# A linear-attention scan and its FFN on one core: the first six stages as a list of interleaved steps, loads held behind FFN groups, k and r of stage 0 in float32

## The chip, the core and the metric

The kernel runs on one core of a Trainium2 chip. The core has a tensor engine (PE, whose weight loads the profile lists apart as PEld), a vector engine (DVE), a scalar engine (ACT), GpSimd (POOL) and a sync engine (SP); each works off its own instructions in order. DMA transfers are issued by SP, ACT or POOL. The metric is the device time of one execution in microseconds; for the kernel before, three runs were taken.

## What is computed

An RWKV-5 style recurrence over 768 tokens for 4 batches and 8 heads of width 48, then a two-layer FFN with leaky ReLU (384 to 2048 to 384) on the 3072 tokens:

```python
for t in range(S):
    cur = np.einsum('bhd,bhe->bhde', u[None] * kt, vt)
    y[:, :, t] = np.einsum('bhd,bhde->bhe', rt, state + cur)
    state = w[None, :, :, None] * state + np.einsum('bhd,bhe->bhde', kt, vt)
...
h = x @ w_in
g = np.maximum(0.01 * h, h)
return g @ w_out
```

Inputs and output are float32.

## The kernel before

The tokens are cut into chunks of 128: 6 chunks in each of 4 batches, 24 *stages* in all, numbered 0 to 23. Weights stay in SBUF. Each stage goes through these steps, most of them one function of the kernel:

- Load: `load_stage(n)` issues three DMAs from POOL's queue, k, r and v of the chunk, float32 in memory and bfloat16 in SBUF.
- `prep(n)` (DVE, lines 267 and 269): k times a table `ktab` of powers of w, r times `qtab`, into `qk`. From stage 6 on (`TURNED`), a DMA transpose on SP's queue turns `qk` into `tp` (line 272).
- `prep2(n)` (DVE, lines 279 to 285): k times u, times r, summed over each head, times v, into `vs` (the diagonal term with u).
- `turn(n)`, stages 0 to 5 only: PE turns `qk` by eight products with an identity into two PSUM banks (line 299), k half first, and ACT copies each half to `tp` (line 305).
- `a_mm(n)` (PE, line 316): the scores, into `ps_at`; `a_mask(n)` (DVE, line 324): times the causal mask, into `at`, two operations.
- `kv_mm(n)` (PE, line 334) and `state(n)` (DVE, lines 346 to 351): the state at the end of the chunk. The last chunk of a batch has none. Its decay table `wl` comes from ACT (lines 253 and 256).
- `y_mm(n)` (PE, line 380), 40 products (28 in the first chunk of a batch), needs `at`, `vs`, `tp` and the state; ACT copies the result to `xT` (line 390).
- `g1(n, grp)`, four *FFN groups* per stage: 12 products on PE (line 401) into one of four PSUM banks, then the leaky ReLU on ACT (line 406). The four banks go round between `turn`, `g1` and `g2`.
- `g2(n)`: 16 products on PE (line 415), a copy on ACT (line 421), the output DMA on SP (line 423).

`Sched.add` records an operation with the keys it reads and writes; each engine then runs its operations in the order in which they were recorded, and waits come from the latest recorded writer of a key. A key that has no writer yet gives no wait. The order of the recording is written out by hand: lines of calls for stages 0 to 5, in blocks (a stage's attention as a whole, then FFN groups), and a loop for stages 6 to 23. The three DMAs of a later load read the key `("pace", n - 6, 0)`, which group 0 of `g1(n - 6)` writes. They are all recorded ahead of `g1_all(5)`:

```python
    for n in range(7, NST):
        load_stage(n, pace=[("pace", n - 6, 0)])
    stage_in(7)
    g1_all(5)
```

In the text a step is named by a letter and its stage: P `prep`, Q `prep2`, T `turn`, A `a_mm`, M `a_mask`, K `kv_mm`, S `state`, Y `y_mm` with its copy, G `g1` (G0.2 is group 2 of stage 0), H `g2`, L `load_stage`.

Of the kernel before, what the change touches and what calls it, by code (L numbers as in the profile page):

```python
# [111 lines left out]
def bass_rwkv5_eagle__then__act_leaky_relu_kernel(  # L112
# [63 lines left out]
    def load_w():  # L176
        def small():
            with nc.allow_non_contiguous_dma(reason="columns of w"):
                return SP.dma_start(wcol[0:D, :], dram(w, 0, [[1, D], [2 * D, NP]]))

        def small2():
            with nc.allow_non_contiguous_dma(reason="columns of w"):
                return SP.dma_start(wcol[64:64 + D, :], dram(w, D, [[1, D], [2 * D, NP]]))

        add("sp", lambda: SP.dma_start(lnw[:, :], dram(w, 0, [[0, 128], [1, HD]])), W=["lnw"], dma="lnw")
        add("sp", lambda: SP.dma_start(u_f[:, :], dram(u, 0, [[0, 128], [1, HD]])), W=["u_f"], dma="u")
        add("sp", small, R=["wcol0"], W=["wcol"], dma="wc")
        add("sp", small2, R=["wcol0"], W=["wcol2"], dma="wc2")

# [38 lines left out]
    load_stage(1)  # L228
    load_stage(2)
    for g in range(3):  # L230
        load_win(g)
    load_stage(3)
    load_win(3)
    load_stage(4)
    for i in range(4):
        load_wout(i)
    load_stage(5)
    load_stage(6)
# [9 lines left out]
    add("dve", lambda: V.tensor_copy(u_tab[:, :], u_f[:, :]), R=["u_f"], W=["u_tab"])  # L248

# [14 lines left out]

    def prep(n):
        iq = n % NQK
        add("dve", lambda: V.tensor_tensor(qk[iq][:, H:2 * H, 0:D], hd(k_sb[:, n, :]), hd(ktab[:, :]), ALU.mult),  # L267
            R=[("k", n), "ktab", ("qk0", iq)], W=[("kp", iq)])
        add("dve", lambda: V.tensor_tensor(qk[iq][:, 0:H, 0:D], hd(r_sb[:, n, :]), hd(qtab[:, :]), ALU.mult),
            R=[("r", n), "qtab", ("qk0", iq)], W=[("qp", iq)])  # L270
# [6 lines left out]
    def prep2(n):  # L277
        i2, iv = n % 2, n % NVS
        add("dve", lambda: V.tensor_tensor(ku[i2][:, :], k_sb[:, n, :], u_tab[:, :], ALU.mult),
            R=[("k", n), "u_tab"], W=[("ku", i2)])  # L280
        add("dve", lambda: V.tensor_tensor(rku[i2][:, :], r_sb[:, n, :], ku[i2][:, :], ALU.mult),
            R=[("r", n), ("ku", i2)], W=[("rku", i2)])
        add("dve", lambda: V.tensor_reduce(s_tok[i2][:, :], hd(rku[i2][:, :]), AX.X, ALU.add),  # L283
            R=[("rku", i2)], W=[("s", i2)])
        add("dve", lambda: V.tensor_tensor(hd(vs[iv][:, :]),  # L285
                                           v_sb[:, n, :].rearrange("p (h e) -> p h e", e=E)[:, :, 0:D],
                                           s_tok[i2][:, :].unsqueeze(2).to_broadcast([128, H, D]), ALU.mult),
            R=[("v", n), ("s", i2)], W=[("vs", iv)])

    def turn(n):  # L290
        it, iq = n % NTP, n % NQK
        for half in (1, 0):
            pb = bank[0] % 4
            bank[0] += 1

            def emit(half=half, pb=pb):
                for p in range(NP):
                    h0 = half * H + 2 * p
                    last = PE.matmul(ps_g[pb][:, 128 * p:128 * p + 128],  # L299
                                     qk[iq][:, h0:h0 + 2, :].rearrange("p h e -> p (h e)"), ident[:, :],  # L300
                                     start=True, stop=True)
# [3 lines left out]
            add("act", lambda half=half, pb=pb: A.activation(  # L305
                tp[it][:, NP * half:NP * half + NP, :].rearrange("p m t -> p (m t)"), ps_g[pb][:, :], AF.Copy),
                R=[("ps_g", pb)], W=[("tp", it, half)])
# [257 lines left out]
```

## Time and profile before

| | us |
|---|---|
| median of 3 runs | 189.87 |
| lowest and highest | 189.8, 190.95 |
| the profiled execution, its own time | 192.09 |
| its span, first to last instruction | 190.3 |

| engine | busy us in the span | share |
|---|---|---|
| PE | 167.7 | 88% |
| PE weight load | 132.0 | 69% |
| DVE | 103.7 | 54% |
| ACT | 92.3 | 48% |
| POOL | 70.0 | 37% |

The chain of work that ended last is 83% PE, 7% DMA, 5% ACT and 2% DVE. A line number is that of the kernel before. In a row of the profile, `out<-in` names what is written and read, `x8` is a count, and what stands in brackets behind a row is the idle time before it and what ended that.

### The profile page before, as it was taken

Reading aid. Unit: us, or ns where it says so; the run is one execution under the profiler, and the core shown is the slowest. Engines: PE = TensorE matmul, PEld = TensorE weight load, DVE = VectorE, ACT = ScalarE, POOL = GpSimd, SP = SyncE. Lnnn points to the kernel's source line nnn. Section 1 sums busy time; section 2 is a strip of 40 time slices with the busy share of each in tenths; the row PEclk is TensorE's granted clock in tenths of the full one; section 3 lists DMA queues with packets and bytes.
Section 4 is the critical chain, followed back from the end, with each engine's and each line's share of the span. In section 5 each row is a group of like instructions: output and inputs, shape, how many; then the busy total and the mean of one; then the engine's idle time right before and its main releaser. Section 6 shows DMA issues by size and latency. Waiting matters only on the chain.

```text
span 190.3 us, 6193 instructions
## 1 busy us (share of the span) xinstructions
PE 167.7 (88%) x2768; PEld 132.0 (69%) x2768; DVE 103.7 (54%) x240; ACT 92.3 (48%) x164; POOL 70.0 (37%) x87
## 2 busy tenths in 40 slices
PE   0266697789798599999999999999999999999993
PEld 0145596687475488778877877887788778778851
DVE  5498810880566665955675577558645955240000
ACT  2732277665344165356436643653475356436621
POOL 7999996059999999800000000000000000000000
PEclk9999999999999789999999999999999999999999
DMA  4999999999999999999937413430442146201112
GB/s 66 124 142 180 170 185 198 145 136 79 154 107 195 150 169 142 168 168 152 156 58 100 100 40 61 100 85 15 100 96 75 28 96 71 70 3 45 41 45 83
DMA packets 101786, 20.46 MB, mean 108 GB/s; under 512 B 94848, under 2 KB 101760, under 8 KB 101760
## 3 DMA queue, kind: packets, MB, share of 16 engines
q0 software_dynamic: 78592, 10.23, 82.8%
q1 hardware_dynamic: 23168, 9.84, 27.3%
q8 instruction: 22, 0.36, 0.9%
q14 instruction: 4, 0.03, 0.0%
HBM read 20.84 MB, written 4.72 MB: 134 GB/s over the span
## 4 chain that ended last, share of the span: by engine, by line
PE 83%; DMA 7%; ACT 5%; DVE 2%; issue 1%; SPq 0%; DVEq 0%; ACTq 0%; POOLq 0%
PE ps_g L401 34%; PE ps_g L415 32%; PE ps_y L380 9%; PE ps_at L316 5%; DMA tp<-qk 4%; ACT tp L305 3%; DMA k_sb<-in_k_dram 3%; PE ps_kv L334 2%; DVE at L324 2%; PE ps_g L299 1%; ACT xT L390 1%; ACT out_sb L421 1%; ACT gT L406 0%; DVE qk L267 0%; SPq L423 0%
## 5 line engine op out<-in xcount | busy, mean ns | idle before, releaser
L401 PE MATMUL ps_g<-xT,w_in_sb 128*128 128x128 bf16 x1152 | 71.0, 224 | 0.8 <-ACT xT L390 0.8
L401 PEld LDWEIGHTS ps_g<-xT,w_in_sb 128*128 128x128 bf16 x1152 | 68.8, 100 | 3.7 <-ACT xT L390 0.8
L415 PE MATMUL ps_g<-w_out_sb,gT 128*128 128x384 bf16 x384 | 66.1, 326 | 0.0
L406 ACT ACTIVATE gT<-ps_g 128x512 bf16<-128x512 f32 x96 | 57.3, 597 | 14.2 <-PE ps_g L401 7.1
L324 DVE TENSOR_TENSOR at<-ps_at,mask 128x512 bf16<-128x512 f32 x48 | 30.9, 686 | 58.0 <-PE ps_at L316 58.0
L415 PEld LDWEIGHTS ps_g<-w_out_sb,gT 128*128 128x128 bf16 x384 | 36.2, 98 | 22.6
L421 ACT ACTIVATE out_sb<-ps_g 128x384 f32<-128x384 f32 x24 | 11.8, 490 | 57.0 <-PE ps_g L415 57.0
L198 POOL DMA_DIRECT2D k_sb<-in_k_dram x24 | 24.1, 1002 | 9.6 <-PE ps_g L401 8.8
L198 POOL DMA_DIRECT2D v_sb<-in_v_dram x24 | 24.2, 1008 | 0.0
L198 POOL DMA_DIRECT2D r_sb<-in_r_dram x24 | 24.0, 1001 | 0.0
L390 ACT ACTIVATE xT<-ps_y 128x384 bf16<-128x384 f32 x24 | 11.8, 490 | 19.6 <-PE ps_y L380 19.4
L380 PE MATMUL ps_y<-at,v_sb 128*32 128x128 bf16 x384 | 16.0, 234 | 2.9 <-DVE at L324 2.9
L316 PE MATMUL ps_at<-tp 48*128 48x128 bf16 x192 | 10.2, 229 | 8.0 <-ACT tp L305 5.6
L380 PE MATMUL ps_y<-ident,vs 128*32 128x128 bf16 x288 | 15.9, 233 | 0.0
L380 PEld LDWEIGHTS ps_y<-at,v_sb 128*32 128x32 bf16 x384 | 10.8, 101 | 6.0 <-DVE at L324 3.6
L285 DVE TENSOR_TENSOR vs<-v_sb,s_tok 128x384 bf16<-128x384 bf16 x24 | 13.4, 558 | 0.8
L283 DVE TENSOR_REDUCE s_tok<-rku 128x8 f32<-128x384 bf16 x24 | 13.3, 553 | 0.8
L316 PEld LDWEIGHTS ps_at<-tp 48*128 48x128 bf16 x192 | 5.8, 98 | 11.4 <-ACT tp L305 6.9
L380 PE MATMUL ps_y<-tp,st 128*32 128x128 bf16 x240 | 13.3, 228 | 0.0
L299 PE MATMUL ps_g<-ident,qk 128*128 128x128 bf16 x48 | 5.1, 264 | 8.0 <-DVE qk L267 8.0
L380 PEld LDWEIGHTS ps_y<-ident,vs 128*32 128x32 bf16 x288 | 10.7, 104 | 0.0
L299 PEld LDWEIGHTS ps_g<-ident,qk 128*128 128x128 bf16 x48 | 3.7, 117 | 8.8 <-issue 8.1
(35 smaller groups left out, 93.5 us busy)
## 6 DMA issues: line engine op xcount, KB each, us to landing
out_dram<-out_sb SPq DMA_DIRECT2D x24, 192.0 KB, 2.2
k_sb<-in_k_dram POOLq DMA_DIRECT2D x24, 96.0 KB, 10.4
r_sb<-in_r_dram POOLq DMA_DIRECT2D x24, 96.0 KB, 10.9
v_sb<-in_v_dram POOLq DMA_DIRECT2D x24, 96.0 KB, 11.8
w_in_sb<-in_moe_w_in_dram POOLq DMA_DIRECT2D x4, 384.0 KB, 8.0
w_out_sb<-in_moe_w_out_dram POOLq DMA_DIRECT2D x4, 384.0 KB, 12.6
tp<-qk SPq DMA_TRANSPOSE x18, 4.5
lnw<-in_w_dram SPq DMA_DIRECT2D x1, 192.0 KB, 4.2
```

What stands on the lines that cost most here:

```text
L198: add("pool", lambda: G.dma_start(dst, src), R=pace, W=[(which, n)], dma=f"{which}{n}")
L283: add("dve", lambda: V.tensor_reduce(s_tok[i2][:, :], hd(rku[i2][:, :]), AX.X, ALU.add), R=[("rku", i2)], W=[("s", i2)])
L285: add("dve", lambda: V.tensor_tensor(hd(vs[iv][:, :]), v_sb[:, n, :].rearrange("p (h e) -> p h e", e=E)[:, :, 0:D], s_tok[i2][:, :].unsque ...
L299: last = PE.matmul(ps_g[pb][:, 128 * p:128 * p + 128], qk[iq][:, h0:h0 + 2, :].rearrange("p h e -> p (h e)"), ident[:, :], start=True, sto ...
L316: last = PE.matmul(ps_at[hh][:, 128 * p:128 * p + 128], tp[it][rows, NP + p, :], tp[it][rows, p, :], start=True, stop=True)
L324: add("dve", lambda hh=hh: V.tensor_tensor(at[n % NAT][:, hh, :, :], ps_at[hh][:, :].rearrange("p (m i) -> p m i", i=128), mask[:, :].unsq ...
L380: last = PE.matmul(ps_y[32 * q:32 * q + 32, 128 * s:128 * s + 128], a, m, start=first_mm, stop=last_mm)
L390: add("act", lambda: A.activation(xT[n % NXT][:, :, :].rearrange("p s t -> p (s t)"), ps_y[:, 0:HD], AF.Copy), R=["ps_y"], W=[("xT", n % N ...
L401: last = PE.matmul(ps_g[pb][:, 128 * f:128 * f + 128], w_in_sb[:, s, 128 * fb:128 * fb + 128], xT[n % NXT][:, s, :], start=s == 0, stop=s ...
L406: add("act", lambda: A.activation(gT[n % NG][:, 4 * grp:4 * grp + 4, :].rearrange("p f t -> p (f t)"), ps_g[pb][:, :], AF.Lrelu), R=[("ps_ ...
L415: last = PE.matmul(ps_g[pb][:, 0:HD], gT[n % NG][:, s, :], w_out_sb[:, s, :], start=s == 0, stop=s == NFB - 1)
L421: add("act", lambda: A.activation(out_sb[io][:, :], ps_g[pb][:, 0:HD], AF.Copy), R=[("ps_g", pb)], W=[("o", io)])
```

## The change

Four things change.

1. The calls for stages 0 to 5 become a list of steps, `ORDER`, recorded from left to right; the loop for stages 6 to 23 records the same steps as before. The first loads become a list too, `LOADS`, with parts of w_in earlier, among the loads of stages 1 to 3.
2. `load_stage(n)` of stages 8 to 23 is recorded behind the FFN groups of stage n - 6 (`L8` to `L11` in the list, the others in the loop), so that the key it reads has a writer. The loads of stages up to 7 have no hold.
3. k and r of stage 0 go to two new float32 tiles, k by SP's queue, r by ACT's; `prep(0)` and `prep2(0)` read those.
4. Smaller ones: the second half of `turn(0)` is copied by DVE; the decay table is computed behind the first half's copy and followed by the load of ACT's table for the leaky ReLU; the copy of u to bfloat16 moves into `prep2(0)`.

```diff
+FIRST, LAG, LOADED = 6, 2, 7
+LOADS = """k1 r1 v1 wi0 wi1 k2 r2 wi2 v2 wi3 k3 r3 v3 wo0 wo1 k4 r4 v4 wo2 wo3 k5 r5 v5 k6 r6 v6 k7 r7 v7"""
+ORDER = """
+P0 K0 T0 Q0 A0 S0 P1 M0 T1 Q1 P2 K1 A1 Y0 M1 G0.0 T2 S1 G0.1 Y1 G0.2 Q2 G1.0 A2 G1.1 M2 K2 P3 G1.2 Y2 T3 S2 G0.3 K3 G1.3
...
-    load_w()
-    load_one(0, "k")
+    add("sp", lambda: SP.dma_start(lnw[:, :], dram(w, 0, [[0, 128], [1, HD]])), W=["lnw"], dma="lnw")
+    load_first("k")
+    add("sp", lambda: SP.dma_start(u_f[:, :], dram(u, 0, [[0, 128], [1, HD]])), W=["u_f"], dma="u")
+    load_wcol(0)
+    load_wcol(1)
...
+            if n == 0 and half == 0:
+                add("dve", lambda dst=dst, pb=pb: V.tensor_copy(dst, ps_g[pb][:, :]),
+                    R=[("ps_g", pb)], W=[("tp", it, half)])
...
+    def decay_table():
+        add("act", lambda: A.activation(wcol[:, :], wcol[:, :], AF.Ln), R=["wcol0", "wcol", "wcol2"], W=["wcol"])
...
+        add("act", lambda: A.preload_act_table(AF.Lrelu))
+
     def state(n):
+        if n == 0:
+            decay_table()
...
+    steps = {"P": prep, "Q": prep2, "T": turn, "A": a_mm, "M": a_mask, "K": kv_mm, "S": state, "Y": y_part,
+             "G": g1, "H": g2, "L": lambda n: load_stage(n, pace=[("pace", n - 6, 0)])}
+    for name in ORDER.split():
+        steps[name[0]](*(int(x) for x in name[1:].split(".")))
+    for n in range(FIRST, NST):
         for grp in range(4):
             g1(n, grp)
...
+        if n + 6 > LOADED and n + 6 < NST:
+            load_stage(n + 6, pace=[("pace", n, 0)])
```

Three places show what the list does to an engine's order. The first is PE behind Y2: in the kernel before, the first FFN products (`xT,w_in_sb`, nine groups of 12 in one piece) follow, then T3, A3, K3 and three more groups.

```order
L401 MATMUL ps_g<-xT,w_in_sb 128x128 x108
L299 MATMUL ps_g<-ident,qk 128x128 x8
L316 MATMUL ps_at<-tp 128x128 x8
L334 MATMUL ps_kv<-v_sb,qk 128x96 x4
L401 MATMUL ps_g<-xT,w_in_sb 128x128 x36
```

The same place, behind Y2, in the kernel after: T3, G0.3, K3, G1.3, A3, then G2.0 and G2.1.

```order
L308 MATMUL ps_g<-ident,qk 128x128 x8
L426 MATMUL ps_g<-xT,w_in_sb 128x128 x12
L347 MATMUL ps_kv<-v_sb,qk 128x96 x4
L426 MATMUL ps_g<-xT,w_in_sb 128x128 x12
L329 MATMUL ps_at<-tp 128x128 x8
L426 MATMUL ps_g<-xT,w_in_sb 128x128 x24
```

So single FFN groups now stand between a turn, the scores and the state product of one stage; six groups (G0.0 to G0.2 and G1.0 to G1.2) have gone ahead of this place. At the very start of PE's order the kernel after has K0, T0, A0, T1, K1, A1 and then Y0, where before Y0 came ahead of T1.

The second place is DVE from P0 to the first mask (`at0`). Before:

```order
L267 TENSOR_TENSOR qk0<-k_sb,ktab 128x8x48
L269 TENSOR_TENSOR qk0<-r_sb,qtab 128x8x48
L279 TENSOR_TENSOR ku0<-k_sb,u_tab 128x384
L281 TENSOR_TENSOR rku0<-r_sb,ku0 128x384
L283 TENSOR_REDUCE s_tok0<-rku0 128x8
L285 TENSOR_TENSOR vs0<-v_sb,s_tok0 128x384
L324 TENSOR_TENSOR at0<-ps_at0,mask 128x512
```

After:

```order
L274 TENSOR_TENSOR qk0<-k0_f,ktab 128x8x48
L276 TENSOR_TENSOR qk0<-r0_f,qtab 128x8x48
L316 CAST tp0<-ps_g1 128x512
L286 CAST u_tab<-u_f 128x384
L288 TENSOR_TENSOR ku0<-k0_f,u_tab 128x384
L290 TENSOR_TENSOR rku0<-r0_f,ku0 128x384
L292 TENSOR_REDUCE s_tok0<-rku0 128x8
L294 TENSOR_TENSOR vs0<-v_sb,s_tok0 128x384
L370 TENSOR_TENSOR st1<-ps_kv,wl 128x384
L274 TENSOR_TENSOR qk1<-k_sb,ktab 128x8x48
L276 TENSOR_TENSOR qk1<-r_sb,qtab 128x8x48
L337 TENSOR_TENSOR at0<-ps_at0,mask 128x512
```

Two copies, the state of stage 0 and P1 have moved ahead of the mask.

The third is SP's queue from the last start-up load to the transpose of stage 8 (`tp2<-qk1` is that of stage 6, `tp3<-qk2` of stage 7, `tp0<-qk3` of stage 8). Before:

```order
L183 DMA wcol<-in_w_dram 48x4x1
L423 DMA out_0_dram<-out_sb0 128x384
L272 DMA_TRANSPOSE tp2<-qk1 128x8x128
L423 DMA out_0_dram<-out_sb1 128x384
L423 DMA out_0_dram<-out_sb2 128x384
L272 DMA_TRANSPOSE tp3<-qk2 128x8x128
L272 DMA_TRANSPOSE tp0<-qk3 128x8x128
```

After:

```order
L189 DMA wcol<-in_w_dram 48x4x1 x2
L279 DMA_TRANSPOSE tp2<-qk1 128x8x128
L448 DMA out_0_dram<-out_sb0 128x384
L279 DMA_TRANSPOSE tp3<-qk2 128x8x128
L448 DMA out_0_dram<-out_sb1 128x384
L448 DMA out_0_dram<-out_sb2 128x384
L279 DMA_TRANSPOSE tp0<-qk3 128x8x128
```

The transposes of stages 6 and 7 stand one and two output transfers earlier. On POOL the change is one of waits alone: before, the issues of stages 7 to 10 each have a wait on PE and those of 11 to 23 have none; after, stages 8 to 23 have one each.

More of the change, by code (lines that the diff above doesn't have):

```diff
@@ L174, in dram, with load_wcol, emit, load_first @@
         return bass.AP(tensor=h.tensor, offset=h.offset + offset, ap=pattern)
-    def load_w():
-        def small():
+    def load_wcol(hh):
+        def emit():
             with nc.allow_non_contiguous_dma(reason="columns of w"):
[L179 to L188, printed above, removed]
+                return SP.dma_start(wcol[64 * hh:64 * hh + D, :], dram(w, hh * D, [[1, D], [2 * D, NP]]))
+        add("sp", emit, R=["wcol0"], W=[f"wcol{1 + hh}"], dma=f"wc{hh}")
+    def load_first(which):
+        src = {"k": k, "r": r}[which][0].rearrange("h t d -> t h d")[0:L, :, :]
+        dst = {"k": k0_f, "r": r0_f}[which]
+        eng = {"k": "sp", "r": "act"}[which]
+        queue = {"k": SP, "r": A}[which]
+        add(eng, lambda: queue.dma_start(dst[:, :].rearrange("p (h d) -> p h d", d=D), src),
+            W=[(which, 0)], dma=f"{which}0")
     def load_one(n, which, pace=()):
@@ L227, in bass_rwkv5_eagle__then__act_leaky_relu_kernel @@
                                         fill=0.0, base=-1, channel_multiplier=-1), R=["ones"], W=["mask"])
[L228 to L238, printed above, removed]
+    for name in LOADS.split():
+        if name[:2] == "wi":
+            load_win(int(name[2:]))
+        elif name[:2] == "wo":
+            load_wout(int(name[2:]))
+        else:
+            load_one(int(name[1:]), name[0])
     for i in range(NQK):
@@ L263, in hd, with k_of, r_of @@
         return x.rearrange("p (h d) -> p h d", d=D)
+    def k_of(n):
+        return k_sb[:, n, :] if n else k0_f[:, :]
+    def r_of(n):
+        return r_sb[:, n, :] if n else r0_f[:, :]
     def prep(n):
         iq = n % NQK
[L267 removed]
+        add("dve", lambda: V.tensor_tensor(qk[iq][:, H:2 * H, 0:D], hd(k_of(n)), hd(ktab[:, :]), ALU.mult),
             R=[("k", n), "ktab", ("qk0", iq)], W=[("kp", iq)])
[L269 removed]
+        add("dve", lambda: V.tensor_tensor(qk[iq][:, 0:H, 0:D], hd(r_of(n)), hd(qtab[:, :]), ALU.mult),
             R=[("r", n), "qtab", ("qk0", iq)], W=[("qp", iq)])
@@ L277, in prep2 @@
     def prep2(n):
+        if n == 0:
+            add("dve", lambda: V.tensor_copy(u_tab[:, :], u_f[:, :]), R=["u_f"], W=["u_tab"])
         i2, iv = n % 2, n % NVS
-        add("dve", lambda: V.tensor_tensor(ku[i2][:, :], k_sb[:, n, :], u_tab[:, :], ALU.mult),
+        add("dve", lambda: V.tensor_tensor(ku[i2][:, :], k_of(n), u_tab[:, :], ALU.mult),
             R=[("k", n), "u_tab"], W=[("ku", i2)])
-        add("dve", lambda: V.tensor_tensor(rku[i2][:, :], r_sb[:, n, :], ku[i2][:, :], ALU.mult),
+        add("dve", lambda: V.tensor_tensor(rku[i2][:, :], r_of(n), ku[i2][:, :], ALU.mult),
             R=[("r", n), ("ku", i2)], W=[("rku", i2)])
@@ L340, in kv_mm @@
         add("pe", emit, R=[("kp", iq), ("v", n), ("qk0", iq)], W=["ps_kv"])
+    def decay_table():
+        add("act", lambda: A.activation(wcol[:, :], wcol[:, :], AF.Ln), R=["wcol0", "wcol", "wcol2"], W=["wcol"])
+        for hh in range(2):
+            rows = slice(64 * hh, 64 * hh + D)
+            add("act", lambda rows=rows, hh=hh: A.activation(
+                wl[rows, :, hh * D:hh * D + D], wcol[rows, :].unsqueeze(2).to_broadcast([D, NP, D]), AF.Exp,
+                scale=float(L)), R=["wcol", "wl"], W=[f"wl{hh}"])
+        add("act", lambda: A.preload_act_table(AF.Lrelu))
     def state(n):
+        if n == 0:
+            decay_table()
         kv = ps_kv[:, 0:HD].rearrange("p (m e) -> p m e", e=2 * D)
@@ L506, in bass_rwkv5_eagle__then__act_leaky_relu_kernel @@
-    g2(NST - 2)
-    g2(NST - 1)
+        if n + 6 > LOADED and n + 6 < NST:
+            load_stage(n + 6, pace=[("pace", n, 0)])
+        if n + 2 < NST:
+            a_mm(n + 2)
+            a_mask(n + 2)
+        if n + 1 < NST:
+            y_part(n + 1)
+            if (n + 1) % NC < NC - 1:
+                kv_mm(n + 1)
+                state(n + 1)
+        g2(n - LAG)
+        if n + 4 < NST:
+            prep(n + 4)
+            prep2(n + 4)
+    for n in range(NST - LAG, NST):
+        g2(n)
```

97 lines of the change are left out of this document (12 added, 85 removed).

## Prediction

> **What bounds the kernel now.** First the busy time of each engine by stretch of the span, then the rate of the FFN's first products by microsecond, then the chain that ended last, in order of time. The first view (length; PE, PEld, DVE, ACT and POOL busy with counts; granted clock; DMA):
>
> ```profile
> 8.00:22.80 14.80, 9.68 (x170) 6.82 (x171) 13.11 (x31) 4.40 (x9) 14.80 (x19) 1.00 1.79 162
> 22.80:45.00 22.20, 19.36 (x363) 18.19 (x363) 10.56 (x25) 16.18 (x28) 13.39 (x16) 1.00 2.02 157
> 45.00:65.00 20.00, 16.47 (x215) 11.08 (x213) 10.35 (x24) 6.53 (x13) 20.00 (x25) 0.98 1.99 142
> 65.00:190.00 125.00, 122.11 (x2026) 95.83 (x2024) 66.31 (x150) 61.36 (x110) 15.01 (x18) 0.99 0.73 88
> ```
>
> From 65 us on PE is busy 122.1 of 125 us: nothing is to be had there. Up to 65 it idles 5.1, 2.8 and 3.5 us in three stretches, after a start of 8 us. And a busy PE is not always a fast one. The same view for line 401 alone, three single microseconds:
>
> ```profile
> 23.80:24.80 1.00, 1.00 (x12) 1.00 (x10) 1.00 2.62 144
> 27.80:28.80 1.00, 1.00 (x21) 1.00 (x19) 1.00 1.32 199
> 66.00:67.00 1.00, 1.00 (x12) 1.00 (x11) 0.50 1.54 216
> ```
>
> 12 products touch a microsecond at a granted 0.50 (66 us), 21 at 1.00 (27.8 us; one that straddles an end counts too), and again 12 at 23.8 us, where the view also says 1.00. So I read the first 26 us as half clock, whatever that column shows. Now the chain (start, length, what):
>
> ```profile
> 1.31 6.00 DMA k_sb<-in_k_dram
> ...
> 7.45 0.37 DVE qk L267
> ...
> 7.95 0.60 PE ps_g L299 x4
> ...
> 9.82 0.63 PE ps_at L316 x8
> ...
> 10.54 1.30 DVE at L324 x2
> ...
> 11.88 0.94 PE ps_y L380 x28
> ...
> 13.40 1.09 ACT tp L305 x2
> ...
> 16.53 1.26 PE ps_y L380 x40
> ...
> 22.77 8.01 PE ps_g L401 x108
> ...
> 56.40 7.07 DMA tp<-qk
> ...
> 65.38 3.88 PE ps_g L401 x48
> ...
> 73.14 2.68 PE ps_g L401 x48
> 75.82 0.33 PE ps_at L316 x8
> 76.15 0.67 PE ps_y L380 x40
> 76.82 0.28 PE ps_kv L334 x4
> 77.09 2.60 PE ps_g L415 x16
> ...
> 187.45 0.49 ACT out_sb L421
> ```
>
> Up to 22.8 us PE hands to ACT, ACT to PE, PE to DVE, and nothing else is in PE's queue: stages 0 to 2 in 15 us. At 56.4 us a DMA transpose sits on the chain, and after that wait 48 products take 3.88 us and not 2.68, which is the half clock again. From 73 us on one stage is 2.68 + 0.33 + 0.67 + 0.28 + 2.60 = 6.56 us, gapless. The last instruction of PE ends 190.3 - 187.4 = 2.9 us before the span does.
>
> **The work that stays.** At full clock PE needs 24 x 6.56 = 157.4 us, about 1.4 less for the eight chunks at the ends of batches that lack a part, and about 3.0 more for six stages of turning on PE (0.5 each, a little less than half of the half-clock row's 2 x 0.60): 159.0 us. The change removes none of it. Before spends 187.4 - 7.95 = 179.4 us on it, so 20.4 us are waits and half clock. The question is how much of that goes.
>
> **The front of the change, step by step.** Rows for DVE and PE's kv product, with their durations (second number):
>
> ```profile
> 6.31 0.46 DVE L248 CAST u_tab<-u_f 128x384 bf16<-128x384 f32 x1 [2.62 <-DMA u_f<-in_u_dram]
> ...
> 8.38 0.35 DVE L279 TENSOR_TENSOR ku<-k_sb,u_tab 128x384 bf16<-128x384 bf16 x1
> 8.76 0.36 DVE L281 TENSOR_TENSOR rku<-r_sb,ku 128x384 bf16<-128x384 bf16 x1
> 9.15 0.55 DVE L283 TENSOR_REDUCE s_tok<-rku 128x8 f32<-128x384 bf16 x1
> 9.74 0.56 DVE L285 TENSOR_TENSOR vs<-v_sb,s_tok 128x384 bf16<-128x384 bf16 x1
> 10.54 1.29 DVE L324 TENSOR_TENSOR at<-ps_at,mask 128x512 bf16<-128x512 f32 x2 [0.24 <-PE ps_at L316]
> ...
> 12.28 0.55 DVE L346 TENSOR_TENSOR st<-ps_kv,wl 128x384 bf16<-128x384 f32 x1
> ```
>
> ```profile
> 10.36 0.50 PE L334 MATMUL ps_kv<-v_sb,qk 128*128 128x96 bf16 x4
> ```
>
> Loads. The lines of the DMA view end in the time from issue to landing. The first two are issues in the first 2.4 us (lnw at 0.81), the third is stage 5's k, issued as the first row behind the fence shows, the last are issues between 70 and 80 us. Behind them, of the timeline, the issue of stage 5's k and the table load on ACT; of the stretches, 15 to 20 us; and of the list of waits (us in total, times, longest) PE's one wait for a transpose.
>
> ```profile
> lnw<-in_w_dram SPq DMA_DIRECT2D x1, 192.0 KB, 4.2
> ...
> k_sb<-in_k_dram POOLq DMA_DIRECT2D x1, 96.0 KB, 6.0
> ...
> k_sb<-in_k_dram POOLq DMA_DIRECT2D x1, 96.0 KB, 14.2
> ...
> k_sb<-in_k_dram POOLq DMA_DIRECT2D x4, 96.0 KB, 15.2
> ```
>
> ```profile
> 21.24 0.98 POOL L198 DMA_DIRECT2D k_sb<-in_k_dram  x1
> ...
> 23.32 1.28 ACT L406 ACT_TABLE_LOAD   x1
> ```
>
> ```profile
> 15.00:20.00 5.00, 3.29 (x64) 2.40 (x60) 4.39 (x10) 1.58 (x3) 5.00 (x7) 1.00 1.44 179
> ```
>
> ```profile
> PE ps_at L316 <- DMA tp<-qk: 2.4, 1, 2.4
> ```
>
> - k0 and r0 by SP's and ACT's queues: no row has such a transfer in float32 there. Issued at 0.8 to 1.3 us, they land after 4.2 to 6.0 us by these rows, so at 5 to 7.3 us. I take 6.5. It buys little, because K0 now stands ahead of T0 on PE and waits for v0. v0 moves up to where k0 stood in POOL's queue, so I give it k0's landing, 1.31 + 6.0 = 7.3 us. All of PE is queued behind it. K0 7.4 to 7.9, T0 to 9.05 (two times 0.6).
> - Four DVE operations of stage 0 read float32. Bounds 0.35 us (bfloat16 row) and 0.55 us (the row with an f32 operand). I take 0.55: +0.8 us on DVE.
> - The copy of T0's second half on DVE: between the 0.46 us cast and half of 1.29 us. 0.65, so tp0 is whole at 9.75 and A0 runs 9.8 to 10.4, as before (9.82).
> - Then DVE has u_tab 0.46, ku and rku 1.1, the sum 0.55, vs 0.56, the state 0.55 and P1 0.55 to 0.6 ahead of the mask that before came next. With 0.04 between them: P1's first half is there at 13.6, the mask of stage 0 ends at 15.2 (before: 11.84).
> - The wcol loads sit behind k0 on SP, and the decay table and the table load (1.28 us, before at 23.3) stand on ACT behind T0's first half, done near 11.3. ACT's next job is T1 at 14.2: nothing late next.
> - PE: T1 13.6 to 14.75, its copies 1.09 on ACT to 15.35, K1 meanwhile, A1 15.4 to 16.0, Y0 0.94 to 16.95, xT0 at 17.45. So **Y0 is 4 us later than before**, but FFN group G0.0 starts at 17.5 and not at 22.8, and from here PE has work at hand: G0.0 1.3 at half clock (twice a quarter of 2.68), T2 to 19.9, G0.1 to 21.2, Y1 1.26 to 22.45. Its mask: DVE after 15.2 has Q1 1.95, P2 0.55, M1 1.3, so 19.0, in time.
>
> At 22.45 us PE has then done what takes 5.0 us at full clock (three turns 1.5, K and A of two stages 1.0, Y0 and Y1 1.2, two FFN groups 1.34). 159.0 - 5.0 = 154.0 us are left.
>
> **When does the clock rise?** In the trace 3.9 us after the first unbroken work (22.7 to 26.6 us). From 17.5 that gives 21.4, so the last 1.05 us before 22.45 run at double rate: -0.5 us.
> The Trainium skill, "TensorE: Matmul & The Clock Gate" (Part 1: The HAM clock gate), says that the gate opens after one busy window of about 3.4 us and that the windows run free of the kernel, so the rise would come between one and two windows after 17.5, by estimate 20.9 to 24.3 us; by it the sum is between 0.3 us less and 1.4 us more. The trace's 3.9 us lie inside that.
>
> **From 22.5 to 50 us.** Per stage PE has 0.5 + 0.33 + 0.17 + 0.67 + 2.68 = 4.35 us, DVE 0.55 + 1.95 + 1.3 + 0.9 = 4.7. DVE starts this part ahead (after M1 at 19.0 come S1 and Q2, done at 21.9), so the masks end near 25.1, 29.8 and 34.5, and PE comes to the Y that needs them near 25.3, 29.7 and 34.7. I allow 0.6 us of waits in all. Loads: stage 5's k was issued at 21.24 and took 14.2, so 35.4; with two transfers fewer ahead of it (two issues of 0.9) it lands about 33.5, and P5 wants it at 34.5. All of w_out stands ahead of it, so it is there too when H0 starts near 37.
>
> **The holds.** Before, loads 11 to 23 were not held, and POOL issued without a pause (20.0 of 20 us, and 15.0 us more after 65, so to 80 us). Now each set of three waits in POOL's queue for its FFN group, and every later load stands behind. Issue (3 x 0.9) plus the worst landing, 15.2, is 18 us; from group 0 of stage n to the point where DVE wants stage n+6 (after g2 of iteration n+2) lie 2 x 6.56 + 5.9 = 19 us. Enough even so, and the queue will be emptier. What they buy: the transposes meet fewer loads. tp7 stood behind the out-transfer of H2 on SP; now only behind that of H0. PE reaches A6 near 49 and A7 near 53, with P6 and P7 at 38 and 41: 7.1 us (the row at 56.4) fit. tp8 is the tight one: P8 follows the mask of 6 (51.0), and A8 comes near 58.2, 7.2 us later.
>
> **Sum.** 22.45 + 154.0 - 0.5 + 0.6 = 176.55, plus 2.9 at the end: a span of 179.5 us, 10.8 less than 190.3. The profiled execution took 192.09 us, 1.8 of it outside the span, 2.2 more than the median of 189.87; I take the difference from the median: **179.1 us**. If that 2.2 is an accident of the profiled execution and not of each, the same span means 181.3.
>
> **Rivals.**
> - *Half clock lasts two windows longer* (0.12). PE's gaps at 13 to 17.5 are like those before, where 3.29 us busy in 5 (15 to 20 us) did not raise it. 6.8 us at half rate cost 3.4: 182.5.
> - *It rises a window earlier*, on T1, K1, A1, Y0 (0.07): -1.7, 177.4.
> - *A transpose is late* (0.10): tp8 or tp7. The price is that of the one before: 2.4 us of wait and 3.88 - 2.68 = 1.2 of half clock: 183.
> - *DVE becomes the bound* of stages 2 to 5 (0.06): if the float32 operations or waits of DVE put each mask 1.5 us behind PE, four times: 185.5. Against it: PE has FFN groups in between.
> - *Other side: the holds make loads late* (0.03). DVE waits in order for k, so masks and PE stop. From a landing of 19 - 2.7 = 16.3 us on each further us is lost once; it needs 27 us to eat the 10.8, and the row of the full queue has 15.2.
>
> The chance that the change does not reorder as it says is nil for PE. The chance that k0 and r0 land no earlier is large, but they are not in the sum.
>
> **Numbers.** 179.1 with 0.62 (177.5 to 181.3). With the rivals up to 184 and down to 176.8 some 0.9 is held; I leave the bound there for the unknown landings. Faster by over 1% (below 188.0) 0.94, within 1% 0.03, slower 0.03; 1% is about what a measurement of this kernel can tell from no change.
>
> **What would show it.** Right: first PE work near 7.4 on ps_kv, A0 no earlier than 9.5, DVE without a pause from 9 to 19 us, the first FFN group near 17.5, 21 products per us from 21 to 24 us on, no transpose in the chain, PE idle under 1 us between 22 and 60, POOL issuing till about 150 us. Wrong: v0 landing after 9 us, half rate past 26 us, PE waiting for the mask or for tp8.

## The result, and the profile after

The kernel after takes 182.74 us (median of 4 runs, 181.74 to 183.06), the kernel before 190.41 in the same comparison (189.8 to 192.51): a ratio of 0.957, 95% interval 0.948 to 0.966. It is faster by 4.3%. The time lies 3.6 us above the number that was forecast: outside the range that was given with a chance of 0.62 (177.5 to 181.3), inside the wider one that goes up to 184. The profiled span is 180.0 us, where 179.5 was forecast. Spans leave out what lies around the first and last instruction, and the steps are compared in them. A ratio leaves out executions that took over 1.5% more than the fastest of their kernel.

First the chain that ended last in the kernel after (start, length, what). The first rows to Y1, then H0 and the rows around the place where the kernel before waited for a transpose:

```profile
1.41 7.05 DMA v_sb<-in_v_dram
...
8.60 0.48 PE ps_kv L347 x4
9.07 0.87 PE ps_g L308 x8
...
9.97 0.69 DVE tp L316
...
13.21 0.55 DVE st L370
...
14.08 0.62 PE ps_g L308 x4
14.72 1.09 ACT tp L319 x2
...
15.96 0.61 PE ps_at L329 x8
16.57 0.90 PE ps_y L404 x26
...
18.12 1.44 PE ps_g L426 x12
...
21.37 0.67 PE ps_y L404 x40
```

```profile
37.90 2.60 PE ps_g L440 x16
...
53.86 0.33 PE ps_at L329 x8
54.19 4.80 PE ps_g L426 x84
58.98 0.33 PE ps_at L329 x8
...
62.86 2.68 PE ps_g L426 x48
```

The front reads as the list writes it: K0, T0, A0, then a row of DVE work of which the state of stage 0 (L370) is the last that is shown here, T1, A1, Y0, and at 18.12 the first FFN group. From 53.86 on A7, seven FFN groups and A8 (at 58.98) follow one another with no transfer between them. The row at 62.86 is the one that stood at 73.14 before, and from either row the same 114.2 us lead to the end of PE's work (187.4 and 177.1), so the whole gain is made ahead of it. About half of it is made before H0: that starts at 37.90 and not at 44.83, but with 17 FFN groups ahead of it and not 20, so of the 6.9 us three groups (2.0) have only moved. The other half lies between H0 and that row, where the transpose was waited for. That transpose, of stage 7, has not become faster. Its issue on SP and its time from issue to landing in the kernel after:

```profile
41.48 1.82 SPq L279 DMA_TRANSPOSE tp<-qk  x1
```

```profile
tp<-qk SPq DMA_TRANSPOSE x1, 7.6
```

In the kernel before it was issued at 56.40 and landed after 7.1 us. The transposes of stages 6 and 8 took 7.0 and 6.8 us, and 6.8 and 7.0 before. PE no longer waits because the list issues the transposes of stages 6 and 7 12 and 15 us earlier, while PE comes to A7 only some 7 us earlier (at 53.86, where it came at 61.2 and waited 2.4).

Next the busy times of the kernel after in the same stretches as before (length; PE, PEld, DVE, ACT, POOL; clock; DMA):

```profile
8.00:22.80 14.80, 9.46 (x155) 8.16 (x156) 11.42 (x25) 6.93 (x13) 14.80 (x18) 1.00 1.81 179
22.80:45.00 22.20, 21.92 (x412) 18.21 (x410) 16.77 (x39) 14.55 (x27) 12.49 (x15) 1.00 2.17 161
45.00:65.00 20.00, 20.00 (x341) 15.54 (x339) 14.38 (x33) 10.06 (x19) 6.32 (x8) 1.00 1.22 129
```

PE is no busier than before in the first stretch (9.46 and 9.68 us). Afterwards it idles 0.3 us and nothing, where it was 2.8 and 3.5. Last, two single microseconds of line 426, and the waits of PE (total, times, longest):

```profile
20.40:21.40 1.00, 0.97 (x12) 0.79 (x10) 1.00 2.49 168
...
22.10:23.10 1.00, 1.00 (x20) 1.00 (x19) 1.00 1.53 192
```

```profile
PE ps_kv L347 <- DMA v_sb<-in_v_dram: 8.6, 1, 8.6
PE ps_g L308 <- DVE qk L274: 2.7, 1, 2.7
```

G0.1, at 20.41, still runs at 12 products per microsecond for the most part; Y1, at 21.37, takes 0.67 us, the full rate, where Y1 before took 1.26. No wait for a transpose is in the list.

### The profile page after: what moved, and what is told of

The parts are those of the page before. It is cut to its first block, busy times and chain, and to the rows that moved or that the text cites. A ratio compares the mean times of both kernels' runs of the same rounds, so it can differ in the third digit from the quotient of the medians.

```text
span 180.0 us, 6182 instructions
## 1 busy us (share of the span) xinstructions
PE 163.5 (91%) x2768; PEld 129.2 (72%) x2768; DVE 105.0 (58%) x241; ACT 90.9 (51%) x163; POOL 68.4 (38%) x85
## 4 chain that ended last, share of the span: by engine, by line
PE 90%; DMA 4%; DVE 2%; ACT 1%; issue 1%; POOL 0%; POOLq 0%; ACTq 0%
PE ps_g L426 37%; PE ps_g L440 35%; PE ps_y L404 9%; PE ps_at L329 4%; DMA v_sb<-in_v_dram 4%; PE ps_kv L347 3%; PE ps_g L308 2%; ACT tp L319 1%; DVE tp L316 0%; DVE rku L290 0%; DVE ku L288 0%; DVE s_tok L292 0%; DVE st L370 0%; ACT xT L415 0%; ACT out_sb L446 0%
## 5 line engine op out<-in xcount | busy, mean ns | idle before, releaser
L426 PEld LDWEIGHTS ps_g<-xT,w_in_sb 128*128 128x128 bf16 x1152 | 67.1, 99 | 4.1 <-issue 0.9
L440 PEld LDWEIGHTS ps_g<-w_out_sb,gT 128*128 128x128 bf16 x384 | 36.3, 98 | 22.5
L209 POOL DMA_DIRECT2D k_sb<-in_k_dram x23 | 20.8, 902 | 62.1 <-PE ps_g L426 52.2
L209 POOL DMA_DIRECT2D v_sb<-in_v_dram x24 | 22.2, 923 | 0.4 <-issue 0.4
L209 POOL DMA_DIRECT2D r_sb<-in_r_dram x23 | 20.9, 907 | 0.0
L404 PE MATMUL ps_y<-ident,vs 128*32 128x128 bf16 x288 | 15.0, 223 | 0.3 <-issue 0.3
L404 PE MATMUL ps_y<-at,v_sb 128*32 128x128 bf16 x384 | 15.0, 225 | 0.0
L347 PE MATMUL ps_kv<-v_sb,qk 128*128 128x96 bf16 x80 | 7.2, 215 | 8.6 <-DMA v_sb<-in_v_dram 8.6
L404 PE MATMUL ps_y<-tp,st 128*32 128x128 bf16 x240 | 12.4, 219 | 0.0
L347 PEld LDWEIGHTS ps_kv<-v_sb,qk 128*128 128x128 bf16 x80 | 4.4, 101 | 10.1 <-DVE qk L276 8.6
L373 DVE TENSOR_TENSOR sum_t<-ps_kv,st 128x384 bf16<-128x384 f32 x16 | 8.8, 549 | 1.3 <-PE ps_kv L347 1.3
```

The source lines that it names most:

```text
L209: add("pool", lambda: G.dma_start(dst, src), R=pace, W=[(which, n)], dma=f"{which}{n}")
L347: last = PE.matmul(ps_kv[:, 96 * p:96 * p + 96], qk[iq][:, H + 2 * p:H + 2 * p + 2, :].rearrange("p h e -> p (h e)"), v_sb[:, n, :].rearra ...
L404: last = PE.matmul(ps_y[32 * q:32 * q + 32, 128 * s:128 * s + 128], a, m, start=first_mm, stop=last_mm)
L426: last = PE.matmul(ps_g[pb][:, 128 * f:128 * f + 128], w_in_sb[:, s, 128 * fb:128 * fb + 128], xT[n % NXT][:, s, :], start=s == 0, stop=s ...
L440: last = PE.matmul(ps_g[pb][:, 0:HD], gT[n % NG][:, s, :], w_out_sb[:, s, :], start=s == 0, stop=s == NFB - 1)
```

## Experiments

A time is a median of 4 to 6 executions. Experiments 1 to 4, 5 to 7 and 8 to 10 are three groups, each on a chip of its own, with runs of the kernel before beside them. Where a median is compared with that of the kernel after, the spans stand beside it, since the times lie 1.7 to 2.9 us above the spans from run to run.

**1. The holds alone.** The kernel before, with the holds recorded behind their FFN groups; nothing else of the change.

```diff
-    for n in range(7, NST):
+    for n in range(7, 11):
         load_stage(n, pace=[("pace", n - 6, 0)])
     stage_in(7)
     g1_all(5)
+    load_stage(11, pace=[("pace", 5, 0)])
...
     for n in range(6, NST):
         g1_all(n)
+        if n + 6 < NST:
+            load_stage(n + 6, pace=[("pace", n, 0)])
```

> The kernel before, with one part of the change: the loads of stages 11 to 23 recorded behind the FFN group they are to wait for. Theory (the list gives most of the gain, the holds only free the transposes): PE's wait for the transpose of stage 7 shrinks from 2.4 us but does not vanish, since on SP it still stands behind the output transfer of H2; the first 45 us stay as they were; the span falls by 1 to 3 us, to 187.3 to 189.3. Rival A (the holds give most): the span falls below 183. Rival B (the holds give nothing): within 0.5 us of 190.3.

Measured: 188.13 us (187.59 to 188.5) against 192.39, ratio 0.980 (0.974 to 0.986); spans 185.7 to 186.5. Its chain, where the kernel before has a transpose of 7.07 us and a stage at half rate:

```profile
55.02 2.68 PE ps_g L401 x48
57.69 0.33 PE ps_at L316 x8
58.02 2.71 PE ps_g L415 x16
60.73 0.33 PE ps_at L316 x8
```

G, A, H, A touch, and the FFN's 48 products take 2.68 us. So the wait goes wholly, though the transpose of stage 7 still stands behind the output transfer of H2 on SP: it is issued at 55.94 and lands after 4.5 us, where it took 7.1 (stages 6 and 8: 4.7 and 5.0, for 6.8 and 7.0). With fewer loads beside them the transposes are faster, and here that is enough without another place on SP. That part of the expectation failed. The 4.2 us by which the profiled spans differ (190.3 and 186.1) are the 3.6 that the prediction gave for one late transpose (2.4 of wait, 1.2 of half clock), and 0.6 more; in the trace of before the half rate lasts from 64.18 to 67.59, so the half of it, 1.7 us, would fit better than the 1.2 of the one row.

**2. The list without holds.** The kernel after; `load_stage` of stages 8 to 23 without its `pace`.

```diff
-             "G": g1, "H": g2, "L": lambda n: load_stage(n, pace=[("pace", n - 6, 0)])}
+             "G": g1, "H": g2, "L": lambda n: load_stage(n)}
...
-            load_stage(n + 6, pace=[("pace", n, 0)])
+            load_stage(n + 6)
```

> The kernel after without any hold on the loads of stages 8 to 23; the list of steps stays. Theory: the first 40 us as after, FFN groups from 18 us on; POOL issues without pause to about 80 us, so the transposes of stages 6 to 8 land later, 5 to 7 us after issue, and cost PE 0 to 3 us; span 180.0 to 183.5. Rival A (the holds give most of the gain): span over 186. Rival B (the holds do nothing for this order): within 0.3 us of 180.0.

Measured: 183.67 us (182.48 to 185.83), ratio 0.952 (0.945 to 0.959); spans 180.7 to 182.8 and, in the execution that was profiled, 184.1. The four of the kernel after lie between 180.0 and 180.8, those of experiment 3, on the same chip, between 180.1 and 181.6. By the ratios the holds can't be told from nothing once the list is there (experiment 3 has 0.952 too); by the medians of the spans (181.4 without 184.1, against 180.15 and 180.45) they may be worth about 1 us. The list alone removes the wait of before: the transposes of stages 6 to 8 land after 7.1, 7.7 and 7.1 us, no faster than in the kernel before, but are issued at 39.94, 42.63 and 52.68, and PE does not wait for them. From stage 9 on the holds do make a difference to them: 8.5 and 7.3 us here, 4.2 and 4.4 in the kernel after. The long execution shows what this can cost, at stage 12:

```profile
84.61 9.89 DMA tp<-qk
...
94.63 0.40 PE ps_at L329 x8
```

A transpose of 9.89 us holds PE up for 2.0. It is one execution, the longest, so this shows that it can happen, not how often.

**3. k and r of stage 0 by POOL again.** The kernel after, with both as bfloat16 from POOL's queue, in the order k, r, v (in it `k_of` and `r_of` give the bfloat16 tiles again).

```diff
-    load_first("r")
...
-    load_first("k")
+    load_one(0, "k")
...
+    load_one(0, "r")
     load_one(0, "v")
...
-        return k_sb[:, n, :] if n else k0_f[:, :]
+        return k_sb[:, n, :]
```

> The kernel after with k and r of stage 0 loaded by POOL in bfloat16 as before, everything else kept. Theory (the float32 loads buy nothing, since PE's first step waits for v0): v0 lands near 8.7 instead of 8.46 us, four DVE operations take 0.35 and not 0.55 us, the span stays within 0.8 us of 180.0. Rival (the early k and r are worth what they seem to be): the first PE work and all behind it about 1.2 us later and the later loads 1.4 us later, span 181.2 or more.

Measured: 182.69 us (182.05 to 183.48), ratio 0.952 (0.945 to 0.959), spans 180.1 to 181.6. That is the kernel after. G0.0 starts at 17.94 and not at 18.12: v lands 0.2 later, behind two transfers, and DVE's products of bfloat16 take less than those of float32. The two float32 tiles are worth nothing that these runs can tell.

**4. Turn first.** The kernel after with T0 ahead of K0 on PE, so that only K0 waits for v.

```diff
-P0 K0 T0 Q0 A0 S0 P1 M0 T1 Q1 P2 K1 A1 Y0 M1 G0.0 T2 S1 G0.1 Y1 G0.2 Q2 G1.0 A2 G1.1 M2 K2 P3 G1.2 Y2 T3 S2 G0.3 K3 G1.3
+P0 T0 K0 Q0 A0 S0 P1 M0 T1 Q1 P2 K1 A1 Y0 M1 G0.0 T2 S1 G0.1 Y1 G0.2 Q2 G1.0 A2 G1.1 M2 K2 P3 G1.2 Y2 T3 S2 G0.3 K3 G1.3
```

> The kernel after with T0 recorded ahead of K0, nothing else. Theory (PE's first step waits for v0 until 8.46 us while qk of stage 0 is ready at 7.2, and DVE's row of work up to the second mask hangs on the turn): first PE work near 7.25, the copy on DVE 1.3 us earlier, the first FFN group at 16.8 and not 18.1 us, span about 178.8, at best 178.4. Rival (the front is hidden, by loads of stage 2 or by the clock's rise at a fixed time): span within 0.3 us of 180.0.

Measured: 180.85 us (180.17 to 181.04), ratio 0.942 (0.936 to 0.948), spans 178.4 to 179.2. On this chip that is 1.8 less than experiment 3, and the two ranges don't meet. From the chain:

```profile
7.15 1.03 PE ps_g L308 x8
...
16.35 1.44 PE ps_g L426 x12
...
50.47 7.45 DMA tp<-qk
...
58.06 0.40 PE ps_at L329 x8
```

G0.0 comes at 16.35, 1.8 earlier. Of that 1.1 is left at H0 (36.78) and 0.8 at the end of the profiled execution: the transpose of stage 8, issued at 50.47, is what A8 waits for now (0.2 us), and the FFN products of stages 2 to 5 pause twice (experiment 6).

**5. Products while PE waits.** Experiment 4, with products of a tile of ones with itself into a bank that the next group overwrites: 56 ahead of T0, 24 behind A0. They add nothing to the output, here and in experiments 8 to 10.

```diff
-P0 T0 K0 Q0 A0 S0 P1
+I56 P0 T0 K0 Q0 A0 I24 S0 P1
...
+    def idle_products(count):
+        def emit():
+            for i in range(count):
+                last = PE.matmul(ps_g[3][:, 0:128], ones[:, :], ones[:, :], start=True, stop=True)
+            return last
+
+        add("pe", emit, R=["ones"], W=[("ps_g", 3)])
```

> T0 ahead of K0 as in the run before, and PE is given 56 products of ones by ones into an unused bank while it waits for stage 0, and 24 more between A0 and T1; their results are overwritten. Theory (PE works at half clock until a stretch of unbroken work has passed, whatever the clock column says for the first 20 us): the clock is full from about 7 us, T0 takes 0.5 and not 1.03 us, the first FFN group 0.67 and not 1.44, Y1 is reached 1 to 2.5 us earlier than in the run with T0 first; the span falls from 179.2 to 177 to 178.5, since the loads of stage 5 take back a part. Rival (the slow products of the front are not clock, but for instance contention with the loads): every duration of the front stays, span 179.2 or more.

Measured: 179.92 us (179.38 to 181.38), ratio 0.939 (0.932 to 0.947), spans 177.6 to 179.7, by their medians 0.45 below experiment 4, on another chip. PE's rows, and the granted clock by stretch:

```profile
8.93 0.40 PE L329 MATMUL ps_at<-tp 48*128 48x128 bf16 x8
...
12.19 0.67 PE L308 MATMUL ps_g<-ident,qk 128*128 128x128 bf16 x8 [1.42 <-DVE qk L274]
...
13.86 0.60 PE L329 MATMUL ps_at<-tp 48*128 48x128 bf16 x8 [0.83 <-ACT tp L319]
```

```profile
10.80:13.90 3.10, 0.88 (x14) 0.72 (x16) 3.03 (x8) 1.09 (x2) 3.10 (x5) 1.00 1.40 196
14.00:20.00 6.00, 5.31 (x88) 4.68 (x88) 5.31 (x13) 2.45 (x5) 6.00 (x8) 0.50 1.76 182
```

A0 takes 0.40 us at 8.93 with the same eight products that A1 takes 0.60 for at 13.86. The loads are the same, and the trace's clock record begins at 7.09 and not at 20.88 as in the kernel after. So the front of the kernels before and after does run at half rate, and products that compute nothing lift it. Then the clock falls: between 10.8 and 13.9 PE is busy for 0.9 of 3.1 us, and from 14 to 20 the column itself says 0.50. In the trace it stays there from 13.92 to 20.74, twice 3.41 us. The Trainium skill, "TensorE: Matmul & The Clock Gate" (Part 1: The HAM clock gate), gives windows of about 3.4 us that run free of the kernel; this length agrees.

**6. Loads and the transpose of stage 8 earlier.** Experiment 4, with k, r and v of stage 5 ahead of the last two parts of w_out, and P8 ahead of Y5. It was to remove the pauses that were left in stages 2 to 5 and before A8.

```diff
-LOADS = """k1 r1 v1 wi0 wi1 k2 r2 wi2 v2 wi3 k3 r3 v3 wo0 wo1 k4 r4 v4 wo2 wo3 k5 r5 v5 k6 r6 v6 k7 r7 v7"""
+LOADS = """k1 r1 v1 wi0 wi1 k2 r2 wi2 v2 wi3 k3 r3 v3 wo0 wo1 k4 r4 v4 k5 r5 v5 wo2 wo3 k6 r6 v6 k7 r7 v7"""
...
-Q3 A3 G2.0 L8 G2.1 M3 Y3 P4 T4 S3 G2.2 G3.0 L9 Q4 A4 G2.3 M4 P5 G3.1 G3.2 Y4 G3.3 K4 S4 G4.0 L10 P6 H0 Q5 T5 G4.1 G4.2 A5 P7 H1 M5
-Y5 H2 G5.0 L11 A6 Q6 M6 P8 G4.3 H3 Y6 Q7 K6 S6 A7 P9 G5.1 M7 G5.2 G5.3 Q8 Q9
+Q3 A3 G2.0 L8 G2.1 M3 Y3 P4 T4 S3 G2.2 G3.0 L9 Q4 A4 G2.3 M4 P5 G3.1 G3.2 Y4 G3.3 K4 S4 G4.0 L10 P6 H0 Q5 T5 G4.1 G4.2 A5 P7 H1 M5 P8
+Y5 H2 G5.0 L11 A6 Q6 M6 G4.3 H3 Y6 Q7 K6 S6 A7 P9 G5.1 M7 G5.2 G5.3 Q8 Q9
```

> T0 ahead of K0, k, r and v of stage 5 loaded ahead of the last two parts of w_out, and P8 recorded two steps earlier, ahead of Y5. Theory (of the 1.8 us that T0 first gained by the first FFN group, 0.3 went to PE's wait near 35 us behind stage 5's loads and 0.2 to 0.3 to the transpose of stage 8): both waits vanish, span 178.5 to 178.9. Rival (they went elsewhere, or H0 now waits for w_out): span 179.2 or more.

Measured: 181.13 us (180.44 to 182.76), ratio 0.945 (0.937 to 0.952), spans 178.7 to 180.0. No gain on experiment 4 (178.4 to 179.2, on another chip). One of the two waits is gone: A8 starts at 58.94, at the end of the FFN groups ahead of it. But the clock rose 1.3 us later in its profile (21.35 and 20.0), and the chain shows that the pauses are no wait for a load:

```profile
29.26 0.68 PE ps_y L404 x38
29.93 0.37 issue
30.30 0.23 PE ps_y L404 x2
...
35.55 0.61 PE ps_g L426 x9
36.16 0.54 issue
36.69 0.33 PE ps_g L426 x3
```

PE stops for 0.37 us between the 38th and the last two products of Y3, whose operands are all there, and for 0.54 in the middle of an FFN group. In the kernel after the first of them stands between the same products, 0.28 us long. A packet of the queue that brings instructions (q8 of the profile) starts some 2 us ahead of each, so I think that PE waits for its own code beside full DMA engines. That was argued from the times, and no run was made on it; against it, other packets of that queue, such as those at 34.25 and 40.09 in the kernel after, are followed by no pause.

**7. Y0 before T1.** Experiment 6 with stage 0 finished first, as in the kernel before.

```diff
-P0 T0 K0 Q0 A0 S0 P1 M0 T1 Q1 P2 K1 A1 Y0 M1 G0.0 T2 S1
+P0 T0 K0 Q0 A0 M0 P1 Y0 S0 T1 Q1 K1 G0.0 A1 M1 P2 T2 S1
```

> As the run with stage 5's loads and P8 moved, and the front in another order: the mask of stage 0 directly behind Q0, Y0 ahead of T1. Theory (DVE's row of work ahead of the first mask is what puts the first FFN group at 16 us): Y0 begins near 12.9 and not 14.8, the first FFN group near 14.4 and not 16.35, and the clock rises about one window earlier at best; span 177.3 to 178.5. Rival (DVE's sum up to the second mask stays the same, so Y1 and all behind it come no earlier): span within 0.3 us of the run with stage 5's loads and P8 moved.

Measured: 184.0 us (183.12 to 185.03), ratio 0.960 (0.951 to 0.968), spans 181.3 to 183.3: on the same chip 2.9 us worse than experiment 6. From its chain:

```profile
14.38 0.49 ACT xT L415
14.87 0.10 ACT wcol L356
...
15.77 0.57 DVE st L370
...
16.38 0.50 PE ps_kv L347 x4
```

The decay table is recorded with S0 and so stands on ACT behind the copy of Y0 now. The state of stage 0 waits for the table, K1 for the state (1.1 us), and G0.0 comes at 16.89 all the same. A1 now stands behind G0.0, so the mask of stage 1 and P2 behind it are late, and T2 waits 1.65 us for P2. Y1 starts at 22.76, where experiment 6 has 20.15. The clock rises at 26.33 and not at 21.35, and the 24 FFN products behind Y1 take 2.60 us for 1.47. So of the 2.9 us, as I read it, the waits ahead of Y1 are the larger part and the later clock about 1.1; the two were not tried apart.

**8. The clock kept.** Experiment 5, with 44 such products behind A0, 12 behind K1 (into the bank of Y0) and 8 behind Y0.

```diff
-I56 P0 T0 K0 Q0 A0 I24 S0 P1 M0 T1 Q1 P2 K1 A1 Y0 M1
+I56 P0 T0 K0 Q0 A0 I44 S0 P1 M0 T1 Q1 P2 K1 I12.1 A1 Y0 I8 M1
```

> As the run with products of ones while PE waits, with more of them: 44 behind A0, 12 behind K1 and 8 behind Y0, so that PE has no pause of a microsecond between 1 and 20 us. Their results are overwritten. Theory (in that run the clock rose at 7.1 us and fell again at 13.9 because PE paused 2.2 us in a row of 5): the clock stays full from about 7 us, the first FFN group starts near 15.0 and takes 0.67 us, Y1 starts near 17.5 and not 19.6; span 176.2 to 177.6. Rival A (the loads of stage 2 and w_in hold the front, whatever the clock): Y1 no earlier than 18.9, span 178 or more. Rival B (the clock falls anyway): G0.0 at half rate, span 178.3.

Measured: 180.32 us (179.53 to 180.53), ratio 0.943 (0.936 to 0.951), spans 177.8 to 178.8. No more than experiment 5, though PE is now at full rate from 5 us to the end (G0.0 in 0.83 us at 15.44, for 1.44). Y1 starts at 18.35, between the 17.5 of the theory and the 18.9 of rival A. The chain and PE's waits say what took over:

```profile
15.38 0.81 POOL k_sb L209
16.20 12.43 DMA r_sb<-in_r_dram
...
28.65 0.37 DVE qk L276
...
29.15 0.43 PE ps_g L308 x4
```

```profile
PE ps_g L308 <- DVE qk L274: 1.8, 4, 0.7
```

PE comes early to the turns, and waits four times for P, whose k and r have not landed. r of stage 4, issued at 16.20, lands at 28.62.

**9. A shorter row on DVE.** Experiment 8 with the copy of u ahead of T0 (step U), both halves of T0 copied by ACT, P1 ahead of S0, and 20 products behind A0, not 44.

```diff
-I56 P0 T0 K0 Q0 A0 I44 S0 P1 M0
+I56 P0 U0 T0 K0 Q0 A0 I20 P1 S0 M0
...
-            if n == 0 and half == 0:
-                add("dve", lambda dst=dst, pb=pb: V.tensor_copy(dst, ps_g[pb][:, :]),
-                    R=[("ps_g", pb)], W=[("tp", it, half)])
```

> As the run with the clock kept, with DVE's row of work ahead of the second mask made shorter: both halves of T0 are copied by ACT, u's copy stands ahead of T0 where DVE waits, P1 stands ahead of S0. Theory (that row, and not PE or the loads, sets when Y1 can run once the clock is full): P1 about 1.4 us earlier, M1 ends about 1 us earlier, span 0.7 to 1.2 us below the run with the clock kept. Rival (the loads bind: r2 lands near 16.4 us and w_in's third part near 18.2): span within 0.3 us of that run.

Measured: 179.78 us (179.34 to 179.89), ratio 0.940 (0.934 to 0.946), spans 177.5 to 178.1: 0.5 us below experiment 8, with ranges that overlap, less than the theory gave (0.7 to 1.2) and more than the rival (0.3). A part of what DVE saves it waits for loads: its waits for k are 3.2 us in all, and 2.6 in experiment 8. Two of its rows, the idle time before them in brackets:

```profile
15.72 0.36 DVE L274 TENSOR_TENSOR qk<-k_sb,ktab 128x384 bf16<-128x384 bf16 x1 [1.16 <-DMA k_sb<-in_k_dram]
...
28.23 0.36 DVE L274 TENSOR_TENSOR qk<-k_sb,ktab 128x384 bf16<-128x384 bf16 x1 [1.07 <-DMA k_sb<-in_k_dram]
```

**10. Loads in order of use.** Experiment 9 with the loads of stages 2, 4 and 5 moved ahead of parts of the weights, and H0 behind A5.

```diff
-LOADS = """k1 r1 v1 wi0 wi1 k2 r2 wi2 v2 wi3 k3 r3 v3 wo0 wo1 k4 r4 v4 wo2 wo3 k5 r5 v5 k6 r6 v6 k7 r7 v7"""
+LOADS = """k1 r1 v1 wi0 k2 r2 wi1 wi2 v2 wi3 k3 r3 v3 k4 r4 v4 wo0 k5 r5 v5 wo1 wo2 wo3 k6 r6 v6 k7 r7 v7"""
...
-G4.0 L10 P6 H0 Q5 T5 G4.1 G4.2 A5 P7 H1 M5
+G4.0 L10 P6 Q5 T5 G4.1 G4.2 A5 H0 M5 P7 H1
```

> As the run with DVE's shorter row, with the loads in the order in which the steps now want them (k2 and r2 ahead of w_in's second part, stage 4 ahead of w_out, stage 5 ahead of its last three parts) and H0 behind A5. Theory (with the clock full and DVE's row short, PE waits for DVE and DVE for k2, r2, k4 and r4, 2.3 us in all between 15 and 30 us): those waits fall below 0.8 us, span 176.2 to 177.2. Rival A (the transfers are the bound as a whole: what one gains another loses, w_in or w_out comes late): span 177.6 or more.

Measured: 179.43 us (178.83 to 179.67, 6 runs) against 192.57, ratio 0.931 (0.928 to 0.934), spans 177.0 to 177.8. This is the lowest median of all, 3.3 us below the kernel after, and 2.55 by the medians of the spans (177.6 and 180.15). It is only 0.35 below experiment 9, whose range it overlaps. The waits did not fall below 0.8 us as expected; PE's have in part moved to the weights:

```profile
PE ps_g L430 <- DMA w_in_sb<-in_moe_w_in_dram: 1.4, 2, 0.9
PE ps_g L306 <- DVE qk L274: 1.2, 2, 0.9
```

What was moved forward made something else late. I read this as rival A: up to 35 us the transfers as a whole bound this version. No run with fewer bytes was made, so that is argued and not shown.

## Why the prediction was right, and where its number was off

The direction and the main mechanism held: FFN groups put between the attention steps, half rate ended early, and no transpose on the chain. The number was luck as far as the wide range goes: 182.74 is near what two of its rivals gave (182.5 and 183), and neither a later clock nor a late transpose came about. By its own steps:

- *K0 waits for v, K0 7.4 to 7.9.* Late by 1.15 us: v landed at 8.46 and not 7.3. Taking k's landing for it was the mistake; here the float32 transfers of k0 and r0 (192 KB each) ran beside it. That these made it late was not tried by itself; in experiment 3, without them but behind two transfers in POOL's queue, it landed at 8.68. T0 ended at 9.94 and not at 9.05, and A0 began at 10.80 and not at 9.8.
- *Float32 operations 0.55, DVE's copy 0.65, the mask of stage 0 at 15.2, T1 at 13.6.* 0.55 to 0.57, 0.69, the mask's end at 15.5, and T1 at 14.08. The row of DVE work up to T1 began 0.9 late and took 4.1 us where 4.5 was forecast (u's copy, for one, took 0.35 and not 0.46), so T1 was late by 0.5 only.
- *G0.0 at 17.5, clock at 21.4, Y1 to 22.45 less 0.5.* 18.12, the rise at 20.88, and Y1 ending at 22.04, within 0.1 of the forecast's 21.95. That closeness is luck: G0.0 began 0.6 late, T2 took 0.85 us and not 1.1, and the clock rose 0.5 early. The rule by which the rise was forecast did not hold: it came 2.8 us after the start of G0.0 here, 2.9 in experiment 3, 3.7 in experiment 4 and 4.8 in experiment 6, not 3.9. The Trainium skill, "TensorE: Matmul & The Clock Gate" (Part 1: The HAM clock gate), asks for one busy window of about 3.4 us, so by it, as an estimate, work ahead of G0.0 must have counted here; which work does, these runs do not show. Experiment 5 confirms that the front is half clock, which the clock column did not show.
- *0.6 us of waits up to 50 us.* 0.3, and neither a mask nor a load among them. Y2, Y3 and Y4 came at 25.43, 29.94 and 35.47 (25.3, 29.7, 34.7 forecast), H0 at 37.90.
- *The holds: transposes meet fewer loads.* Not where it was needed: the transposes of stages 6, 7 and 8 took 7.0, 7.6 and 6.8 us, as long as before, and only from stage 9 on (4.2, 4.4) are they faster. What freed PE is the other reason that the prediction gave, P6 and P7 early on SP, so that 7.1 us fit; experiment 2 has that without holds. Experiment 1 has the holds without the list, and there they shorten the three to 4.7, 4.5 and 5.0 us, which is enough as well. So either part removes the wait by itself, and the sum, which went by 7.1 us, was right. A6 at 49.37, A7 at 53.86 and A8 at 58.98 were forecast at 49, 53 and 58.2. The tight one was tp8, as said: it held here, and in experiment 4 it cost 0.2 us. A k load lands after 5.4 us in the median in the profile of after and 10.4 in that of before, so the late-load rival was far off.
- *k0 and r0 in float32 buy little.* Experiment 3: nothing that can be told.
- *The work that stays.* From Y1's end to PE's last product the trace has 155.05 us, and 154.0 + 0.6 was forecast: 0.75 us more work, 0.3 less waiting.
- *Small slips of the working.* K is put at 0.17 us from 22.5 us on, where the row shown has 0.28; the trace of after has 0.17 for a K between FFN groups, so this did no harm. Four times 1.5 us on 179.1 is 185.1 and not 185.5. POOL's last issue came at 130.7, not near 150.

Up to here the sum is off by 0.5 us (180.0 against 179.5). **The term that was mis-sized is the last one**, the way from the span to the time: "2.2 more than the median of 189.87; I take the difference from the median". The four executions of after have spans of 180.0 to 180.8 and times 1.7 to 2.9 us above them, so the median of time minus span is 2.3. Taking the difference from the median came to a time 0.4 below the span. As I read it, the 2.2 us were no accident around the profiled execution, they lay in its span; the spans of the three runs behind the median are not on record. The kernel before ran 32 times beside the experiments, and its spans fall into steps by their mean clock: 188.3 to 189.2 us at 1.000, 189.2 to 191.3 at 0.990 or 0.991, 191.4 and more at 0.982. A fall of 3.41 us at half rate, as in the trace of before, takes 0.9% off the mean clock of 190 us, so I read the steps as none, one and two such falls; of 32 runs 7 had none. The profiled execution had one, behind the late transpose (clock 0.991, 190.3 us); runs of 189.87 us, less the 1.8 around a span, stand at 188.1, where there is none. The kernel after has no such fall, and all its clocks are 1.000, so its span had to be set beside its own surroundings. "The same span means 181.3" was the right reading of the two that the sum ended with; from there 0.65 us more of span (the median is 180.15) and 0.5 more around it lead to 182.45, and 0.3 is what medians of three quantities leave open.
